# g's low half on GpSimd, Strassen's products in three pieces, and batch 0's row sums as products with ones, in a fused block-causal attention and gated feed-forward kernel

## The chip, the cores and the metric

The kernel runs on one core of a Trainium2 chip. The metric is the device time of one execution in microseconds (us); the kernel before was run three times: 994.45 us in the median, 994.39 to 995.16.

The engines are named as in the profile: PE (TensorE, matrix products; PEld its weight loads), DVE (VectorE), ACT (ScalarE), POOL (GpSimd), SP (SyncE, which only issues DMAs).

## The reference

Block-causal attention over 8 batches of 8 heads (576 tokens, head size 64, blocks of 64), then a feed-forward layer with a gate, all in float32:

```python
scores = scale * np.matmul(q, k.transpose(0, 1, 3, 2))          # q, k, v: (8, 8, 576, 64)
scores = np.where(block_i >= block_j, scores, -1000000000.0)    # blocks of 64 tokens
scores = scores - np.max(scores, axis=-1, keepdims=True)
attn = np.exp(scores)
attn = attn / (np.sum(attn, axis=-1, keepdims=True) + 1e-09)
x = np.matmul(attn, v)                                          # then heads side by side: (4608, 512)
h = x @ w_in                                                    # w_in: (512, 2048)
g = h * np.clip(h + 3.0, 0.0, 6.0) / 6.0
out = g @ w_out                                                 # w_out: (2048, 512)
```

## The kernel before, in words

**Precision.** Most products are made of three float16 products: each operand is split into a high half and a low half (the rounding rest, scaled), and high x high, high x low and low x high are summed in PSUM. Making a low half is one instruction, `scalar_tensor_tensor` (value times scale minus high half), on DVE; the high half is a scaled copy on ACT or DVE. Batch 0 runs in float32 instead, while the weights are still being loaded and split.

**Attention.** The heads go in pairs n (4 pairs a batch, 32 in all), the nine blocks of 64 queries in three groups g of three. For the pairs of batch 0, `s_pair32` and `s_soft32` make the scores (tile sf), DVE takes the row maximum (st), ACT takes the exponential (tile pf, with the row's sum as its accumulator output, `sums`), `t_block32` transposes on PE (pt, copied to pT) and `pv_group32` multiplies P^T with V (the output is also called pf). There the sums, which lie one to a partition, have to be spread along the free dimension: their reciprocals are put on a diagonal (rd, three small copies on POOL or ACT), and a product of rd with a matrix of ones in two of its quadrants (`halves`, or `cross` for the blocks whose two heads are swapped) gives pr, which is copied to rb and multiplied with pf. For the other batches `s_group` does the same with float16 halves: tiles s, p (exponentials), phl (halves of P, transposed by DMA) and pv in `pv_group`. A memset on POOL clears the half block behind p.

**Feed-forward.** The 4608 rows of x are cut into 13 pieces pc of 384 columns (pieces 0 and 3 have 192), which lie transposed in four buffers xb. For each piece and each of 16 columns f of 128 hidden units, `ffn1` makes h (24 products of 384 columns, 64 output rows each, two at a time), ACT makes r = relu(scaled h + 3), DVE r = min(r, 6) x h, ACT or DVE the high half of g, DVE its low half; `ffn2` multiplies with w_out into three tiles o, LAG = 3 columns later in the program. At the end of a piece ACT or DVE evacuates o to osb, which SP stores.

**Strassen.** In the pieces of STR = (11, 12), `h_pair` makes two columns f from seven products m of half the size instead of eight: 84 products of 192 columns in place of 48 of 384. The sums of quarters of x (`x_comb`) and of the weights (`w_comb`, once, tile ws) are made ahead; the weight sums lie in buffers that attention uses until then (`SW_TAGS`), and pieces in STR start when all attention for all of them is done (`fills`). The seven products are put together by DVE, seven instructions and one copy (hf, hu), before ACT can make r.

**The order.** The kernel does not issue its instructions as it makes them. `Recorder` records each with a due time (`key`, from tables such as AT for attention and FT for the feed-forward), what it depends on, and the engines that could do it; `schedule` then simulates five engines with estimated costs and lets each engine take, among what is ready, what is due first. `emit` issues the result (all from line 520, so the profile tells instructions apart by their tiles). Each engine then works through its own list in that order, and an instruction that waits holds up all behind it on its engine.

## Time and profile before

| what | value |
|---|---|
| median of three runs | 994.45 us |
| the profiled execution's own time | 995.16 us |
| its span, first to last instruction | 993.4 us |
| PE busy | 970.4 us, 98% |
| DVE busy | 889.6 us, 90% |
| ACT busy | 638.6 us, 64% |
| POOL busy | 67.8 us, 7% |
| read from and written to HBM | 45.09 MB, 9.44 MB |

A row that groups instructions ("lines") names the tiles as out<-in without buffer numbers, then the shapes and the count (x), then busy us and the mean ns of one, then the idle time of the engine ahead of them and what ended it. A row of the chain or of the timeline begins with start and length in us from the span's start; x24 counts instructions in the row. A row of waits names who waited for whom, then us in total, times, and the longest. Matmul ends are modelled, so a row of products may reach into the next one by some 0.2 us: where products are costed, it is from one row's start to the next row's.

### The profile page before, as it was taken

How to read it: one execution, taken by the hardware profiler on the slowest of the kernel's cores; microseconds unless marked ns; L12 is line 12 of the kernel's file. 1: busy time of each engine (PE TensorE's matmuls, PEld its weight loads, DVE VectorE, ACT ScalarE, POOL GpSimd, SP SyncE). 2: the span in 40 equal slices, each digit the busy share in tenths (PEclk: the TensorE clock that was granted, in tenths of full speed). 3: DMA queues.
4: the chain of work that ended last, by engine and by line, in shares of the span. 5: the costliest groups of instructions: out<-in, count | busy, mean ns of one | idle time of the engine just before them, and what ended most of it. 6: DMA issues, size and time to landing. Idle time of an engine off the chain costs nothing. (4 is left out here: it accounts for less than half of the span.)

```text
span 993.4 us, 31344 instructions
## 1 busy us (share of the span) xinstructions
PE 970.4 (98%) x12673; PEld 723.0 (73%) x12673; DVE 889.6 (90%) x2441; ACT 638.6 (64%) x1538; POOL 67.8 (7%) x239
## 2 busy tenths in 40 slices
PE   6899999999999999999999999999999999999998
PEld 5566667767778877777677777777667777788876
DVE  5898999999999999999999889899898889976863
ACT  4788887766757776776776665666656555354442
POOL 1132210000000000000000000000000002000000
PEclk9999999999999999999999999999999999999999
DMA  8965479899869989789998876786756551000000
GB/s 235 304 205 164 97 123 147 147 172 197 156 109 204 164 153 156 147 159 165 149 182 137 142 149 111 123 164 120 130 138 110 92 103 36 2 34 2 34 2 33
DMA packets 407041, 129.05 MB, mean 130 GB/s; under 512 B 393968, under 2 KB 396272, under 8 KB 406896
## 3 DMA queue, kind: packets, MB, share of 16 engines
q1 hardware_dynamic: 360528, 111.49, 58.9%
q10 hardware_dynamic: 46368, 15.55, 7.1%
q8 instruction: 99, 1.62, 0.7%
q14 instruction: 46, 0.38, 0.1%
HBM read 45.09 MB, written 9.44 MB: 55 GB/s over the span
## 5 line engine op out<-in xcount | busy, mean ns | idle before, releaser
L520 PE MATMUL o<-wout,g 128*64 128x512 f16 (+3 forms) x3336 | 411.1, 378 | 0.0
L520 PE MATMUL h<-x,win 128*64 128x384 f16 (+2 forms) x3952 | 361.7, 319 | 2.1 <-DVE g L520 0.9
L520 PEld LDWEIGHTS <-win 128*64 128x64 f16 (+1 forms) x4440 | 269.0, 110 | 62.7 <-issue 2.9
L520 PEld LDWEIGHTS <-g 128*64 128x64 f16 x3360 | 217.8, 110 | 106.1
L520 ACT ACTIVATE p<-s,st,esc 128x64 f32<-128x64 f32 (+1 forms) x280 | 162.8, 587 | 75.0 <-DVE st L520 62.6
L520 ACT ACTIVATE r<-h,eg,sh 128x384 f32<-128x384 f32 (+1 forms) x192 | 111.6, 599 | 51.6 <-PE h L520 47.9
L520 DVE SCALAR_TENSOR_TENSOR phl<-p,st,phl 128x128 f16<-128x128 f32 (+4 forms) x252 | 135.5, 582 | 0.1
L520 ACT ACTIVATE g<-r 128x384 f16<-128x384 f32 (+1 forms) x156 | 79.1, 507 | 69.2 <-DVE r L520 66.8
L520 DVE TENSOR_REDUCE st<-s 128x1 f32<-128x64 f32 (+1 forms) x280 | 116.9, 446 | 1.2 <-PE s L520 1.1
L520 DVE SCALAR_TENSOR_TENSOR g<-r,g 128x384 f16<-128x384 f32 (+1 forms) x192 | 102.5, 534 | 7.1 <-ACT g L520 5.6
L520 DVE SCALAR_TENSOR_TENSOR r<-r,eg,h 128x384 f32<-128x384 f32 (+1 forms) x160 | 93.9, 587 | 14.2 <-ACT r L520 13.7
L520 PE MATMUL s<-qkT 128*64 128x64 f16 (+7 forms) x1120 | 94.3, 287 | 2.5 <-DVE x L520 1.7
L520 ACT ACTIVATE phl<-p,st 128x256 f16<-128x256 f32 (+4 forms) x135 | 70.6, 557 | 26.9 <-DVE st L520 15.9
L520 PEld LDWEIGHTS <-vhl 128*64 128x64 f16 x1680 | 72.8, 110 | 13.2 <-issue 3.8
L520 PEld LDWEIGHTS <-qkT 128*64 128x64 f16 x1120 | 57.6, 110 | 26.9 <-issue 6.8
L520 PE MATMUL pv<-pT,vhl 128*64 128x192 f16 (+2 forms) x1680 | 73.2, 233 | 1.8 <-DVE x L520 0.8
L520 POOL MEMSET p<- 128x64 f32 x140 | 21.2, 152 | 593.9 <-DVE phl L520 531.0
L520 ACT ACTIVATION_READ_ACCUMULATOR p<-s,st,esc 128x1 f32 x280 | 55.5, 198 | 0.0
L520 ACT ACTIVATE r<-hf,eg,sh 128x192 f32<-128x192 f32 (+1 forms) x48 | 25.5, 591 | 43.2 <-DVE hf L520 43.2
L520 DVE TENSOR_SCALAR phl<-p,st 128x512 f16<-128x512 f32 (+4 forms) x117 | 45.2, 420 | 2.0
L520 DVE SCALAR_TENSOR_TENSOR qks<-qk,rs_q,qks 128x576 f16<-128x576 f32 x56 | 44.8, 815 | 0.0
L520 PE MATMUL m<-x,ws 128*64 128x192 f16 x768 | 35.2, 246 | 0.0
(193 smaller groups left out, 1033.0 us busy)
## 6 DMA issues: line engine op xcount, KB each, us to landing
out_dram<-osb SPq DMA_DIRECT2D x35, 256.0 KB, 2.4
qk<-in_q_dram SPq DMA_DIRECT2D x21, 288.0 KB, 3.8
rawo<-in_moe_w_out_dram SPq DMA_DIRECT2D x10, 512.0 KB, 5.6
vnat<-in_v_dram ACTq DMA_DIRECT2D x36, 128.0 KB, 4.0
qk<-in_k_dram SPq DMA_DIRECT2D x15, 288.0 KB, 4.3
qk<-in_k_dram ACTq DMA_DIRECT2D x13, 288.0 KB, 4.6
vnat<-in_v_dram SPq DMA_DIRECT2D x28, 128.0 KB, 2.9
rawi<-in_moe_w_in_dram SPq DMA_DIRECT2D x6, 512.0 KB, 5.5
```

The lines of the kernel that those rows point to most:

```text
L520: getattr(eng, method)(*args, **kw)
```

## The change

**Row sums.** `s_soft32` no longer takes the exponentials' accumulator output. In `pv_group32` the loop that makes pf runs twice: first with ones (64 columns, `full1`) as the weights into pr, then with V into pf. pr then holds the row sums at the place where pf has its rows; one instruction on DVE or ACT adds 1e-9 and copies it to rb, and DVE takes the reciprocal there (192 columns). sums, ident2, halves, cross and rd go.

**g.** r is scaled through the tables of constants, so that g's high half is a plain copy and its low half a plain difference. From piece 2 on this difference is a `tensor_tensor` on POOL.

**Strassen.** STR is (10, 11, 12). There are five buffers xb, the weight sums use other buffers, and hu uses those of phl2.

**Order.** The tables of due times have other numbers, each group of operations has a shift of its own (`SHIFT`, some 1450 numbers), and the estimated costs differ for POOL; the copies for which POOL was one of several choices now all fall to DVE and ACT.

The diff, cut to its core:

```diff
-STR = (11, 12)
-SK, SKD, XK = 19.373, 8.522, 32.06
+RDB = 3
+GLO = ("P",)
+STR = (10, 11, 12)
+SK, SKD, XK = 23.677, 8.167, 30.349
...
+SHIFT = {
+    0: 118, 2: -43, 3: -76, 4: -56, 5: 114, 6: -70, 7: 29, 8: -137, 11: -65, 12: -176, 13: -47, 14: 115,
...
+    def minus(self, out, a, b, engines):
+
+        self.add([
+            ("vector" if e == "V" else "gpsimd", "tensor_tensor", (out, a, b), dict(op=ALU.subtract))
+            for e in engines
+        ])
...
+            op.grp = self.grp + (10000 if eng == "tensor" else 20000 if ways[0][1] == "dma_start" else 0)
+            op.key += 0.1 * SHIFT.get(op.grp, 0)
...
-            port = len(wide) > 1
+            port = False
...
-            occ = 75 + (2.0 if method == "tensor_tensor" else 1.1) * n
+            occ = 80 + (1.4 if method == "tensor_scalar" else 3.2) * n
...
-    xb = [wpool.tile([P, 2, NDT, TP], F16, tag=f"x{i}", name=f"x{i}") for i in range(4)]
+    xb = [wpool.tile([P, 2, NDT, TP], F16, tag=f"x{i}", name=f"x{i}") for i in range(5)]
...
-            for i, f in enumerate((1.0, 3.0, 6.0)):
+            for i, f in enumerate((E_G, 3.0 * E_G, 6.0 * E_G)):
...
-        for ci, (c0, c1, ps) in enumerate(pss):
-            nc.scalar.activation(
-                pr[:, c0:c1], ps[:, :c1 - c0], AF.Exp, bias=st[:, 0:1], scale=1.0,
-                accum_out=st[:, 2:3] if ci else sm_,
-            )
-        if len(pss) == 2:
-            nc.vector.tensor_add(sm_, sm_, st[:, 2:3])
+        for c0, c1, ps in pss:
+            nc.scalar.activation(pr[:, c0:c1], ps[:, :c1 - c0], AF.Exp, bias=st[:, 0:1], scale=1.0)
...
-        r = sums.pop((n, g))
-        nc.vector.tensor_scalar(r, r, 1e-9, 1.0, op0=ALU.add, op1=ALU.mult)
-        nc.vector.reciprocal(r, r)
-        rd = sm.tile([P, GB, BLK], F32, tag="rd", bufs=2, name=f"rd{n}_{g}")
-        for i in range(GB):
-            nc.scaled(rd[:, i], ident2, r[:, i:i + 1], RDW)
...
-        nc.joint = "pr", n, g
-        for w, b0, b1 in sets:
-            nc.tensor.matmul(
-                pr[:, b0 * BLK:b1 * BLK], (halves, cross)[w], rd[:, b0:b1].rearrange("p i x -> p (i x)"),
-                start=True, stop=True,
-            )
...
+        for what, to in (("pr", pr), ("pf", ps)):
+            nc.joint = what, n, g
+            for w, b0, b1 in sets:
...
+                        nc.tensor.matmul(
+                            to[h * D:(h + 1) * D, i0 * BLK:b1 * BLK],
+                            vnat[n % NVB][:kp, j, h, :] if what == "pf" else full1[:kp],
+                            t[:kp, us, o:o + BLK],
...
+        nc.add([
+            ("scalar", "activation", (rb, pr, AF.Identity), dict(bias=tiny)),
+            ("vector", "tensor_scalar", (rb, pr, 1e-9, 1.0), dict(op0=ALU.add, op1=ALU.mult)),
+        ][::-1])
+        nc.vector.reciprocal(rb, rb)
...
-        nc.scaled(g[:, 0, :w], r[:, :w], E_G, "AV")
-        nc.vector.scalar_tensor_tensor(
-            g[:, 1, :w], r[:, :w], E_G, g[:, 0, :w], op0=ALU.mult, op1=ALU.subtract
-        )
+        nc.scaled(g[:, 0, :w], r[:, :w], 1.0, "AV")
+        nc.minus(g[:, 1, :w], r[:, :w], g[:, 0, :w], GLO[(pc * NFT + f) % len(GLO)] if pc > 1 else "V")
```

What this does to the engines' lists is shown at three places. First PE, at the end of pair 0's batch-0 attention, group 2 (pr0_2 and pf0_2; sf1 are the scores of pair 1, h0_4 a column of piece 0, gs1 belongs to the weights' scales). Before:

```order
L520 MATMUL pr0_2_306<-rd0_2_305,halves_95 128x128
L520 MATMUL pr0_2_306<-rd0_2_305,cross_96 128x64
L520 MATMUL h0_4_316<-x0_81,win_85 128x192 x2
L520 MATMUL sf1_3_0_296<-qkf1_123 64x256 x2
L520 MATMUL sf1_4_0_297<-qkf1_123 64x320 x2
L520 MATMUL gs1_283<-wm1_281,unit_98 64x2 x2
...
L520 MATMUL pf0_2_308<-pT0_2_275,vnat0_100 64x128 x8
L520 MATMUL pf0_2_308<-pT0_2_275,vnat0_100 64x64 x10
```

And now:

```order
L690 MATMUL pr0_2_284<-pT0_2_256,unit_96 64x128 x8
L690 MATMUL pr0_2_284<-pT0_2_256,unit_96 64x64 x10
L690 MATMUL sf1_5_0_296<-qkf1_120 64x384 x2
L690 MATMUL sf1_6_0_297<-qkf1_120 64x448 x2
L690 MATMUL gs1_261<-wm1_259,unit_96 64x2 x2
...
L690 MATMUL h0_4_290<-x0_81,win_86 128x192 x3
L690 MATMUL pf0_2_285<-pT0_2_256,vnat0_99 64x128 x8
L690 MATMUL pf0_2_285<-pT0_2_256,vnat0_99 64x64 x10
```

Two products with rd have become 18 with pT, the same 18 as those of pf, and they stand as far ahead of pf as before.

Second POOL, in the attention of pair 17 (p17 and phl17 are memsets for it, g4 the subtractions for piece 4). Before:

```order
L520 MEMSET p17_0_1346 128x64
L520 MEMSET p17_2_1348 128x64
L520 MEMSET p17_4_1369 128x64
L520 MEMSET phl17_1_1372 128x256
L520 MEMSET p17_6_1389 128x64
L520 MEMSET p17_8_1390 128x64
```

And now:

```order
L690 MEMSET p17_0_1290 128x64
L690 MEMSET p17_2_1292 128x64
L690 TENSOR_TENSOR g4_14_1264<-r4_14_1263,g4_14_1264 128x384
L690 TENSOR_TENSOR g4_13_1253<-r4_13_1252,g4_13_1253 128x384
L690 MEMSET phl17_1_1320 128x256
L690 MEMSET p17_4_1317 128x64
L690 MEMSET p17_6_1336 128x64
L690 TENSOR_TENSOR g4_15_1278<-r4_15_1277,g4_15_1278 128x384
L690 TENSOR_TENSOR g5_0_1285<-r5_0_1283,g5_0_1285 128x384
L690 MEMSET p17_8_1337 128x64
```

The subtractions stand between memsets that wait for DVE to have read the buffer's last contents. Over the whole program POOL has 176 subtractions, 160 of 384 columns and 16 of 192.

Third DVE, around column 4 of piece 5 (r5_4; st are the scores' maxima and scales, qks the halves of q and k, x the halves of x). Before:

```order
L520 SCALAR_TENSOR_TENSOR r5_4_1336<-r5_4_1336,eg8_723,h5_4_1335 128x384
L520 SCALAR_TENSOR_TENSOR x3_84<-pv16_0_1339,x3_84 128x384
L520 TENSOR_SCALAR st17_0_1344<-st17_0_1344,esc17_1296 128x3
L520 TENSOR_SCALAR pw_q18_1359<-am_q18_1361 128x2
L520 TENSOR_REDUCE st17_1_1365<-s17_1_0_0_1366 128x1
L520 SCALAR_TENSOR_TENSOR g5_4_1337<-r5_4_1336,g5_4_1337 128x384
```

And now:

```order
L690 SCALAR_TENSOR_TENSOR r5_4_1328<-r5_4_1328,eg8_688,h5_4_1327 128x384
L690 TENSOR_SCALAR qks19_1362<-qks19_1362 128x2x9x32
L690 TENSOR_SCALAR x2_83<-pv17_0_1346 128x384
L690 TENSOR_SCALAR st18_0_1351<-st18_0_1351 128x3
...
L690 SCALAR_TENSOR_TENSOR x2_83<-pv17_0_1346,x2_83 128x384
```

DVE no longer makes g's low half, and attention is one pair further on (18 and 19 in place of 17 and 18) at the same column of the feed-forward.

More of the change, by code (lines that the diff above doesn't have):

```diff
@@ L592, in pow2_scale @@
         else:
-            pw, rs = (sm.tile([P, n], F32, tag=f"{x}{n}_{nm[0]}", name=f"{x}_{nm}") for x in ("pw", "rs"))
+            pw, rs = (
+                sm.tile([P, n], F32, tag=f"{x}{n}_{nm[0]}", bufs=5 if nm[0] == "v" else 3, name=f"{x}_{nm}") for x in ("pw", "rs")
+            )
         am = sm.tile([P, n], F32, tag=f"am{n}", name=f"am_{nm}")
@@ L628 @@
     make_identity(tc.nc, ident)
-    ident2 = wpool.tile([P, BLK], F32, tag="ident2", name="ident2")
-    nc.vector.tensor_add(ident2, ident[:, :BLK], ident[:, BLK:])
-    halves = wpool.tile([P, P], F32, tag="halves", name="halves")
-    nc.gpsimd.memset(halves, 0.0)
-    for h in range(2):
-        nc.gpsimd.memset(halves[h * BLK:(h + 1) * BLK, h * BLK:(h + 1) * BLK], 1.0)
-    cross = wpool.tile([P, P], F32, tag="cross", name="cross")
-    nc.gpsimd.memset(cross, 1.0)
-    for h in range(2):
-        nc.gpsimd.memset(cross[h * BLK:(h + 1) * BLK, h * BLK:(h + 1) * BLK], 0.0)
     one = wpool.tile([P, 1], F32, tag="one", name="one")
@@ L970, in qk_prep32 @@
         nc.scaled(qT[:, c0:c1], pss[1][:, :c1 - c0], D ** -0.5, "AV")
-    sums = {}
     pf = {}
@@ L1097, in pv_group32 @@
         nj = (3 * g + 2) // 2 + 1
[L1098 to L1115 removed]
+        for what, to in (("pr", pr), ("pf", ps)):
+            nc.joint = what, n, g
+            for w, b0, b1 in sets:
+                js = [j for j in range(nj) if 2 * j - 3 * g < b1]
+                for j in js:
+                    i0 = max(b0, 2 * j - 3 * g)
+                    kp = BLK if 2 * j + 1 > 3 * g + 2 else P
+                    a = i0 * NU[g] + j
+                    us = slice(a, a + (b1 - 1 - i0) * NU[g] + 1, NU[g])
+                    for h in range(2):
+                        o = (h ^ w) * BLK
+                        nc.tensor.matmul(
+                            to[h * D:(h + 1) * D, i0 * BLK:b1 * BLK],
+                            vnat[n % NVB][:kp, j, h, :] if what == "pf" else full1[:kp],
+                            t[:kp, us, o:o + BLK],
+                            start=(j == 0),
+                            stop=(j == js[-1]),
+                        )
+            nc.joint = None
+        rb = sm.tile([P, GT], F32, tag="rb", bufs=2, name=f"rb{n}_{g}")
+        nc.add([
[3 more added lines that the diff above has]
+        nc.vector.reciprocal(rb, rb)
         if g == 0:
@@ L1256, in pv_group @@
         for pc, *_ in parts:
-            while done1 < (pc - 3) * NFT or pc == 2 and done1 < NFT or pc == 3 and done2 < NFT:
+            while (
+                done1 < (pc - 4) * NFT or pc == 2 and done1 < NFT or pc == 3 and done2 < NFT
+                or pc == 5 and done2 < 2 * NFT
+            ):
                 ffn_step(TOT)
@@ L1319, in h_plain @@
     def h_plain(pc, f):
-        x, w, fc = xb[pc % 4], width(pc), f * P % NH
+        x, w, fc = xb[pc % 5], width(pc), f * P % NH
         ps = ps_h.tile([P, TP], F32, tag="h", name=f"h{pc}_{f}")
@@ L1348, in w_comb @@
     def w_comb(c):
-        r = attp.tile([P, NDT, NH], F32, tag="qks", bufs=1, name=f"wr{c}")
-        plus(r, win[:, c, :, 0], win[:, c, :, 1])
+        rs = []
+        for i in range(2):
+            r = attp.tile([P, NDT, P], F32, tag="vhl", bufs=2, name=f"wr{c}_{i}")
+            plus(r, *(win[:, c, :, l, i * P:(i + 1) * P] for l in range(2)))
+            rs += [r[:, :2], r[:, 2:]]
+        a11, a12, a21, a22 = rs
         o = attp.tile([P, 4, 2, P], F32, tag="phl1", bufs=1, name=f"wq{c}")
-        a11, a12, a21, a22 = (r[:, 2 * j:2 * j + 2, i * P:(i + 1) * P] for i in range(2) for j in range(2))
         nc.vector.tensor_add(o[:, 0], a21, a22)
@@ L1358, in w_comb @@
         tag = SW_TAGS[c]
-        pool = {"qk": natp, "raw": ffp}.get(tag, attp)
+        pool = natp if tag == "qk" else attp
         bufs = 2 if tag in ("qk", "qkT", "pT2") else 1
@@ L1732 @@
                 left[pc] += 1
-    for _, _, f, a, key in sorted(ev, key=lambda e: e[:2]):
-        nc.key, nc.cls = key, "w" if f in (load_next, maxes, splits) else "a"
+    for _, no, f, a, key in sorted(ev, key=lambda e: e[:2]):
+        nc.key, nc.cls, nc.grp = key, "w" if f in (load_next, maxes, splits) else "a", no
         f(*a)
```

106 lines of the change are left out of this document (43 added, 63 removed), and 153 rows, old and new, of the table SHIFT.

## The prediction

> **What bounds the kernel now.** I read the busy time of each engine by stretch first, then PE's waits, then the chain that ended last. The columns are start and end of a stretch, its length, then PE, PEld, DVE, ACT and POOL in busy us with the number of instructions, the granted clock (1.00 throughout), the DMA share and GB/s:
>
> ```profile
> 0.00:50.00 50.00, 37.42 (x452) 27.93 (x454) 37.05 (x108) 28.89 (x91) 8.92 (x36) 1.00 0.91 270
> 50.00:250.00 200.00, 196.03 (x2218) 133.12 (x2216) 192.42 (x557) 155.11 (x378) 27.55 (x67) 1.00 0.78 157
> 250.00:850.00 600.00, 597.40 (x7873) 450.49 (x7871) 560.71 (x1548) 396.41 (x956) 31.38 (x137) 1.00 0.76 136
> 950.00:993.40 43.40, 39.59 (x582) 30.38 (x577) 21.68 (x51) 15.00 (x27) 0.00 (x0) 1.00 0.06 20
> ```
>
> PE is idle for 12.6 us of the first 50, for 4.0 us of the next 200, for 2.6 us of the 600 after that, and for 3.8 us at the end, where the last result is evacuated and stored. So PE's own work sets the time, and an edit counts by what it adds to or takes from PE, and by what it does to some 19 us of waits. DVE has little room: 93% busy from 250 to 850 us. PE's longest waits:
>
> ```profile
> PE qt L520 <- DMA qf<-in_q_dram: 4.9, 2, 4.4
> PE sf L520 <- ACT pf L520: 3.7, 3, 1.5
> PE s L520 <- DVE x L520: 1.7, 2, 1.4
> PE pt L520 <- ACT pT L520: 1.4, 1, 1.4
> PE pt L520 <- ACT pf L520: 1.3, 2, 1.1
> ```
>
> The first is the load of q, which the change cannot shorten. The others of batch 0 end with ACT's exponentials (pf) or copies (pT); the one on x ends with DVE, later in the run.
>
> **Strassen for piece 10.** The chain of waits is, in its second half, PE alone, and so shows what a block of products costs:
>
> ```profile
> 858.35 1.95 PE h L520 x24
> 866.13 3.47 PE m L520 x84
> 869.60 3.88 PE o L520 x36
> ```
>
> Two columns f of h cost 2 x 1.95 = 3.90 us as 48 products, and 3.47 us as the 84 half-width products of Strassen's scheme. Piece 10 has eight such pairs: PE loses 8 x 0.43 = 3.4 us, all on the path.
>
> **Row sums of batch 0 on PE.** The new sums are the products of pf once more, with ones in place of V, so their cost is that of pf (the times are from a row's start to the next block's start); the old broadcast pr goes:
>
> ```profile
> 27.75 0.81 PE L520 MATMUL pf<-pT,vnat 128*64 128x128 f32 x12
> 28.50 0.28 PE L520 MATMUL mb_v<-dg_v,one 1*64 1x1 f32 x4
> 28.70 0.49 PE L520 MATMUL pr<-rd,halves 128*128 128x128 f32 x2
> ...
> 29.29 0.58 PE L520 MATMUL sf<-qkf,qkf 64*64 64x128 f32 x8
> ```
> ```profile
> 46.39 1.11 PE L520 MATMUL pf<-pT,vnat 128*64 128x64 f32 x20
> 47.33 0.60 PE L520 MATMUL o<-wout,g 128*64 128x256 f32 x4
> ```
> ```profile
> 54.75 0.39 PE L520 MATMUL pr<-rd,halves 128*128 128x128 f32 x2
> ...
> 55.14 0.87 PE L520 MATMUL h<-x,win 128*128 128x192 f32 x4
> ...
> 57.70 1.82 PE L520 MATMUL pf<-pT,vnat 128*64 128x128 f32 x36
> 59.45 0.33 PE L520 MATMUL pt<-ident,pf 128*128 128x128 f32 x1
> ```
>
> A group of g=0 costs 0.75 us, of g=1 0.94, of g=2 1.75; the old pr costs 0.39 to 0.59 us, 0.49 in the middle. The four pairs' g=0 groups add 4 x (0.75 - 0.49) = 1.0 us, but lie in the first 40 us, where PE idles 12.6 us anyway: I count them at nothing, and 1.0 us if that idle time goes. The other eight groups add 4 x (0.94 + 1.75 - 2 x 0.49) = 6.8 us between 45 and 135 us, where PE has almost no idle time: all of it counts.
>
> What goes with the old sums is on the other engines:
>
> ```profile
> L520 ACT ACTIVATION_READ_ACCUMULATOR pf<-sf,st 128x1 f32 x40 | 8.0, 199 | 0.0
> L520 ACT ACTIVATE rd<-ident,sums 128x64 f32<-128x64 f32 x14 | 4.2, 338 | 0.8 <-DVE sums L520 0.5 <-ACT rb L520 0.3
> ```
>
> ACT loses 40 reads of its accumulator, 8.0 us, and 14 of the diagonal copies rd, 4.2 us; POOL loses the other 22. Such a read stands between each exponential and the transposition that PE waits for. In the first 50 us 12.6 - 4.9 = 7.7 us of PE's idle time are not the first load. The five ended by pf become shorter by at least a read, 5 x 0.2 = 1.0 us; in the other direction all 7.7 us could go. What comes next there is DMA (0.91 busy), so not all of it. I take 5.0 us, most of the 3.7 + 1.3 + 1.4 = 6.4 us that end with ACT, since the groups also lose ACT's and POOL's steps ahead of pr; this is the least certain term. New on DVE are 12 reciprocals of 192 columns. No row shows one over three columns; bounded by the 0.35 us of another 192-column instruction (hf, below) and eight times that, they are 4 to 34 us of DVE, behind a product that nobody on PE waits for soon. I take the lower end.
>
> **g's low half on GpSimd.** The chain of a g, and what four GpSimd subtractions' nearest kin (xr, an addition of the same size) took:
>
> ```profile
> L520 DVE SCALAR_TENSOR_TENSOR g<-r,g 128x384 f16<-128x384 f32 x176 | 96.8, 551 | 6.6 <-ACT g L520 5.1
> L520 DVE SCALAR_TENSOR_TENSOR r<-r,eg,h 128x384 f32<-128x384 f32 x144 | 87.3, 607 | 13.2 <-ACT r L520 12.8
> L520 ACT ACTIVATE r<-h,eg,sh 128x384 f32<-128x384 f32 x112 | 74.4, 666 | 39.2 <-PE h L520 37.5 <-DMA out_dram<-osb 1.3
> L520 ACT ACTIVATE g<-r 128x384 f16<-128x384 f32 x142 | 74.0, 521 | 65.4 <-DVE r L520 63.1
> L520 DVE SCALAR_TENSOR_TENSOR hf<-m,hu 128x192 f32<-128x192 f32 x48 | 15.5, 354 | 3.8 <-PE m L520 0.8
> L520 DVE SCALAR_TENSOR_TENSOR x<-xt,x 128x384 f16<-128x384 f32 x8 | 5.1, 638 | 0.0
> L520 POOL TENSOR_TENSOR xr<-x x4: 1022/1622/3038, 795.8 to 838.4; 128x384 f32<-128x384 f16 x4
> ```
>
> 160 of the 176 wide subtractions leave DVE: 160 x 0.551 = 88 us (16 narrow ones too). Piece 10's assembly brings 7 x 8 x 0.354 = 20 us back. DVE is not the bound, so this saves nothing by itself. It pays for something else: Strassen's weight sums lie in buffers of the attention, so attention must now be done before three Strassen pieces rather than two. One such piece is 8 x (3.47 + 3.88) = 59 us, so DVE has 541 us in place of 600 for what it does from 250 to 850 us. That work is 560.7 us less 120 subtractions (7.5 pieces), 66 us, less piece 10's own r, 16 x 0.607 = 10 us: 485 us, 90% of 541.
>
> Sharing has a price, seen at two of the four additions:
>
> ```profile
> 835.41 4.02 POOL L520 TENSOR_TENSOR xr<-x 128x384 f32<-128x384 f16 x2 [5.12 <-DVE x L520]
> ...
> 838.12 0.54 DVE L520 TENSOR_TENSOR xt<-xt,xr 128x192 f32<-128x192 f32 x1
> 838.59 1.26 DVE L520 SCALAR_TENSOR_TENSOR x<-xt,x 128x384 f16<-128x384 f32 x1
> ```
>
> ```profile
> 827.64 0.75 DVE L520 SCALAR_TENSOR_TENSOR phl<-p,st,phl 128x512 f16<-128x512 f32 x1
> ```
> ```profile
> 829.96 0.89 DVE L520 SCALAR_TENSOR_TENSOR phl<-p,st,phl 128x512 f16<-128x512 f32 x1
> ```
>
> While POOL adds, DVE's x takes 1.26 us, where its mean is 0.64, and its xt 0.54 where 192 columns cost 0.35. The phl that starts inside another addition takes 0.89 us, the one before it 0.75. That is 0.95 us over the four additions, 0.24 us each; and POOL itself needs 1.0 to 3.0 us. With 0.24 us more for each of 120, 29 us, DVE is at 514 us of 541, 95%, little more than now. So the 6.6 us of PE's idle time between 50 and 850 us stay about as they are; I take 2.8 us off, since the waits on DVE's x and g sit in front of the relief, with 0 and 6.6 as ends.
>
> The Trainium skill ("GPSIMD Engine Reference", When to use GPSIMD) speaks against the move: two-input elementwise work belongs on VectorE, GpSimd being about half as fast. The rows agree (1.0 to 3.0 us against 0.55); by itself that rule costs PE nothing, as long as g is early enough.
>
> **The sum.** -3.4 + 6.8 - 5.0 - 2.8 = -4.4 us. The profiled execution took 995.16 us for its span of 993.4, so 990.8; the median of the runs lies 0.7 us lower, so **990.0 us**. With the first two terms fixed and the others uncertain by half their size, this case's own range is 986 to 992.5. About 0.2%, 2 us, is what a measurement of this kernel can tell from no change.
>
> **Rivals.** (1) Slower: g comes late. The chain is 0.67 + 0.61 + 0.52 = 1.80 us up to the high half, then 0.55 us now, up to 3.04 on POOL, where it also queues behind memsets that wait for DVE's phl. In PE's order, priced at the rates above, every g of pieces 2 to 12 now has at least 5.7 us of other products between its h and its first use; after the change 14 of 176 have under 5.5, the least 4.3. With three hand-overs of some 0.3 us (half an instruction in front), the chain is 1.8 + 0.9 + POOL's time: it decides from 2.3 us of POOL on, and at 3.04 makes PE wait 0.7 us in each of 14 places, +10 us: 1000. Against it: the middle xr is 1.6 us, and 110 of the 176 uses are over 10 us away. Chance 0.16. (2) No change: the start is set by its loads, and none of the 5.0 us comes: 995. For it speaks the DMA share of 0.91 there. Chance 0.17. (3) More gain: all 7.7 and 6.6 us of idle time go: 983. Chance 0.11. (4) DVE is held by POOL: at the longest hold seen, 1.26 - 0.64 = 0.62 us for each of 120, DVE needs 485 + 74 = 559 us of 541, and is the bound by 18 us: 1008; it decides from 0.47 us on. Against it: the four held DVE for 0.24 us in the mean. Chance 0.10. The Trainium skill ("SBUF — State Buffer", Who interferes with whom) has this as a rule: a VectorE instruction with two SBUF inputs and a GpSimd instruction that reads SBUF exclude each other, for whole instructions, whoever starts first. By it, the case comes out whenever DVE's next instruction of that kind arrives early in a subtraction.
>
> **How the numbers follow.** The forecast has 0.46. Faster: 0.46 + 0.11 = 0.57; same, rival 2: 0.17; slower: 0.16 + 0.10 = 0.26. The range 982 to 1001 takes in the forecast, rival 2 and the times worked out for 1 and 3, and leaves out 4 and the outer edges of 1 and 3, some 0.2 in all.
>
> **What would show it.** Right: PE does 24 x 84 products m; PE busy in the first 50 us rises above 40; pr costs as much as pf; POOL's g under 2.3 us in the mean and no line of PE waiting for POOL; DVE 90 to 95% busy until attention ends, some 60 us further from the end than now. Wrong: PE waits named on POOL's g (rival 1), DVE at 99% with long phl and x instructions (4), or a first 50 us as idle as before (2).

## The result: slower by 38 us

The changed kernel takes 1032.57 us in the median of four runs (1028.92 to 1038.04), the kernel before 994.42: a ratio of 1.0389, 95% interval 1.0363 to 1.0416. The forecast was 990 us, its range ended at 1001.

The profiled execution took 1030.56 us, its span 1028.8. The busy time by stretch, with the columns as in the prediction (the last stretch now ends at 1028.8):

```profile
0.00:50.00 50.00, 38.98 (x414) 28.04 (x414) 34.62 (x86) 22.23 (x57) 2.07 (x18) 0.86 0.82 240
50.00:250.00 200.00, 192.21 (x2261) 133.75 (x2259) 188.85 (x527) 148.60 (x337) 9.81 (x40) 1.00 0.74 148
250.00:850.00 600.00, 583.58 (x7771) 427.15 (x7768) 560.56 (x1481) 395.20 (x969) 147.29 (x263) 1.00 0.82 140
950.00:1028.80 78.80, 74.93 (x1144) 58.74 (x1138) 39.51 (x102) 29.69 (x55) 18.64 (x20) 1.00 0.06 22
```

PE's idle time from 50 to 850 us has grown from 6.6 to 24.2 us (7.8 + 16.4), and besides the clock is down to 0.86 in the first 50 us. Over the whole span the engines were busy for:

```profile
PE 988.4 (96%) x13185; PEld 727.9 (71%) x13185; DVE 885.4 (86%) x2351; ACT 635.3 (62%) x1495; POOL 203.6 (20%) x366
```

So of the 35.4 us by which the span grew, 17.4 are idle time of PE (40.4 us, 23.0 before), and 18.0 are busy time (988.4 us, 970.4 before). Idle time alone shows half of the loss. No single wait explains it. PE's longest waits now:

```profile
PE s L690 <- ACT p L690: 6.4, 8, 3.1
PE sf L690 <- ACT qkf L690: 4.5, 2, 3.8
PE qt L690 <- DMA qf<-in_q_dram: 3.3, 1, 3.3
PE h L690 <- DVE r L690: 2.7, 4, 1.5
PE pv L690 <- ACT p L690: 2.2, 3, 1.2
```

There are many small ones on attention's chain (s, p, x), and none of PE for POOL's g (PE's weight loads waited for it once, for 0.4 us). Now the groups that the prediction spoke of. PE's row sums, before and after:

```profile
L520 PE MATMUL pr<-rd,halves 128*128 128x128 f32 (+1 forms) x24 | 5.0, 291 | 0.0
L520 PE MATMUL pr<-rd,cross 128*128 128x64 f32 (+1 forms) x24 | 4.4, 266 | 0.0
```
```profile
L690 PE MATMUL pr<-pT,unit 128*64 128x128 f32 (+2 forms) x272 | 16.0, 263 | 0.0
```

DVE's low half of P, before and after, with the new reciprocals, and POOL's subtraction:

```profile
L520 DVE SCALAR_TENSOR_TENSOR phl<-p,st,phl 128x128 f16<-128x128 f32 (+4 forms) x252 | 135.5, 582 | 0.1
```
```profile
L690 DVE SCALAR_TENSOR_TENSOR phl<-p,st,phl 128x256 f16<-128x256 f32 (+4 forms) x252 | 146.3, 622 | 2.0 <-ACT phl L690 1.7
L690 DVE RECIPROCAL rb<-rb 128x192 f32<-128x192 f32 x12 | 16.2, 1348 | 1.9 <-ACT rb L690 1.9
```
```profile
L690 POOL TENSOR_TENSOR g<-r,g 128x384 f16<-128x384 f32 (+1 forms) x176 | 173.1, 989 | 427.1 <-ACT g L690 309.6 <-DVE g L690 55.2 <-DVE pw_q L690 12.7
```

phl has grown from 582 to 622 ns. A reciprocal of 192 columns takes 1.35 us. POOL's subtraction takes 0.99 us in the mean, far below the 2.3 us from which rival 1 decides.

Where does a longer phl come from? From POOL: here is one subtraction, and the phl that VectorE began while it ran (start and length in us):

```profile
255.37 1.36 POOL L690 TENSOR_TENSOR g<-r,g 128x384 f16<-128x384 f32 x1 [5.29 <-DVE phl L690]
```
```profile
255.88 1.40 DVE L690 SCALAR_TENSOR_TENSOR phl<-p,st,phl 128x512 f16<-128x512 f32 x1
```

POOL ends at 256.73, and phl 0.55 us later. The one of the same size that the prediction shows by itself took 0.75 us, this one 1.40: it stood for most of the time for which POOL still ran.

**Theories.** A: the 38 us come through VectorE, which POOL's subtractions hold and which has the reciprocals besides, in stretches where it has no room; PE pays in many small waits. B (rival): the new order itself is at fault, packed so that usual chains come late. C (my prediction's): the reciprocals cost nothing. D: the clock at the start is a part. The expectations split some of these (A1, A2, A', D') and add E, transfers that come late. All results, each against the kernel before on the same chip:

| kernel | what it is | us, median (lowest to highest) | ratio, 95% interval |
|---|---|---|---|
| constant_for_difference | changed, POOL writes zeros | 1010.85 (1009.57 to 1012.62) | 1.0165 (1.0146 to 1.0185) |
| eight_columns | changed, POOL subtracts 8 columns | 1012.96 (1012.10 to 1013.18) | 1.0176 (1.0153 to 1.0199) |
| one_input | changed, POOL scales r | 1017.66 (1014.45 to 1021.46) | 1.0236 (1.0191 to 1.0280) |
| low_half_on_dve | changed, low half on VectorE | 1017.62 (1015.61 to 1019.56) | 1.0226 (1.0202 to 1.0249) |
| before_gpsimd | before, with the subtraction on POOL | 998.38 (996.63 to 999.34) | 1.0038 (1.0024 to 1.0052) |
| copy_for_reciprocal | changed, no reciprocals | 1022.23 (1020.62 to 1026.11) | 1.0284 (1.0256 to 1.0312) |
| no_row_sums | and few products for row sums | 1020.35 (1019.62 to 1022.74) | 1.0257 (1.0234 to 1.0281) |
| before_row_sums | before, with the new row sums | 1026.04 (1023.34 to 1029.65) | 1.0321 (1.0294 to 1.0348) |
| before_row_sums_const | and no reciprocals | 1021.87 (1019.97 to 1025.53) | 1.0281 (1.0258 to 1.0303) |
| all_three | changed: zeros, no reciprocals, few products | 1006.10 (1002.16 to 1009.16) | 1.0108 (1.0072 to 1.0143) |
| dve_no_row_sums | the same with the low half on VectorE | 1010.17 (1007.93 to 1010.39) | 1.0154 (1.0138 to 1.0170) |
| all_three_no_stores | all_three, 33 stores left out | 996.59 (991.28 to 999.78) | 1.0014 (0.9994 to 1.0034) |
| all_three_filled | all_three, early transpositions twice | 998.63 (998.09 to 999.76) | 1.0046 (1.0029 to 1.0063) |
| start_filled | changed, 11 idle products at the start | 1029.79 (1025.92 to 1031.57) | 1.0349 (1.0321 to 1.0378) |
| after_filled | changed, early transpositions twice | 1028.80 (1027.27 to 1032.23) | 1.0356 (1.0332 to 1.0380) |
| dve_filled | low_half_on_dve, the same | 1013.82 (1013.41 to 1014.54) | 1.0200 (1.0185 to 1.0215) |
| no_shift | changed, SHIFT empty | 1062.25 (1057.03 to 1065.58) | 1.0678 (1.0642 to 1.0714) |

### The profile page after: what moved, and what is told of

It is laid out like the page before. It is cut to its first block, busy times and chain, and to the rows that moved or that the text cites. A ratio compares the mean times of both kernels' runs of the same rounds, so it can differ in the third digit from the quotient of the medians.

```text
span 1028.8 us, 32511 instructions
## 1 busy us (share of the span) xinstructions
PE 988.4 (96%) x13185; PEld 727.9 (71%) x13185; DVE 885.4 (86%) x2351; ACT 635.3 (62%) x1495; POOL 203.6 (20%) x366
## 5 line engine op out<-in xcount | busy, mean ns | idle before, releaser
L690 PE MATMUL h<-x,win 128*64 128x384 f16 (+2 forms) x3568 | 328.2, 318 | 3.8 <-DVE r L690 2.7
L690 POOL TENSOR_TENSOR g<-r,g 128x384 f16<-128x384 f32 (+1 forms) x176 | 173.1, 989 | 427.1 <-ACT g L690 309.6
L690 ACT ACTIVATE p<-s,st,esc 128x64 f32<-128x64 f32 (+3 forms) x280 | 163.1, 587 | 53.4 <-DVE st L690 41.4
L690 DVE SCALAR_TENSOR_TENSOR phl<-p,st,phl 128x256 f16<-128x256 f32 (+4 forms) x252 | 146.3, 622 | 2.0 <-ACT phl L690 1.7
L690 DVE TENSOR_REDUCE st<-s 128x1 f32<-128x64 f32 (+3 forms) x280 | 118.0, 444 | 4.6 <-PE s L690 4.4
L690 PE MATMUL s<-qkT 128*64 128x512 f16 (+7 forms) x1120 | 99.1, 288 | 9.7 <-ACT p L690 6.4
L690 ACT ACTIVATE phl<-p,st 128x128 f16<-128x128 f32 (+4 forms) x144 | 76.2, 566 | 39.9 <-DVE st L690 19.5
L690 ACT ACTIVATE r<-hf,eg,sh 128x384 f32<-128x384 f32 (+1 forms) x64 | 36.0, 618 | 63.3 <-DVE hf L690 61.9
L690 PE MATMUL m<-x,ws 128*64 128x192 f16 x1152 | 56.4, 246 | 1.5 <-DVE hu L690 0.8
L690 PEld LDWEIGHTS <-ws 128*64 128x64 f16 x1152 | 50.8, 110 | 5.1 <-issue 1.4
```

The costliest lines, as they stand in the source:

```text
L690: getattr(eng, method)(*args, **kw)
```

## Experiments on GpSimd's subtraction

Most edits stand in `emit`, behind the making of the order, so that every instruction keeps its place.

**constant_for_difference.**

```diff
             for method, args, kw in o.ways[o.eng][0]:
+                if o.eng == "gpsimd" and method == "tensor_tensor":
+                    method, args, kw = "memset", (args[0], 0.0), {}
                 getattr(eng, method)(*args, **kw)
```

> The changed kernel with every instruction in its place, but GpSimd writes zeros where it subtracted, so g's low half is left out of the result; GpSimd no longer reads SBUF there and no longer waits for g's high half. Theory A (VectorE is held by the subtractions: its instructions grew by 34 us in all, 28 of them from attention's phl, st, x, qks and the like, in a stretch where it is 97 to 99% busy): most of that growth goes, phl back from 622 to about 582 ns, and 12 to 20 us of the 38 with it, 1012 to 1020 us. Theory B (the new order packs TensorE's list so tightly that ScalarE's and VectorE's usual chains come late, whoever shares SBUF): 1029 to 1036 us, as the changed kernel's 1032.6.

1010.9 us: 21.7 us less, as A said and B did not. phl is back where it was before:

```profile
L692 DVE SCALAR_TENSOR_TENSOR phl<-p,st,phl 128x256 f16<-128x256 f32 (+4 forms) x252 | 135.8, 582 | 3.3 <-ACT phl L692 2.9
```

VectorE's busy time, with the same 2351 instructions, is 844.6 us instead of 885.4: the holds were 40.8 us, 0.23 us for each of 176 subtractions.

```profile
PE 980.7 (97%) x13185; PEld 729.2 (72%) x13185; DVE 844.6 (84%) x2351; ACT 633.7 (63%) x1495; POOL 99.5 (10%) x366
```

PE's busy time falls by 7.7 us too, with the same 13185 products. A product's row is longer than PE's pace (a row of h is 326 ns long, but 24 of them take 1.95 us, 81 ns each), so a shorter wait between two products leaves no idle time. That the 7.7 us are such waits is inferred.

**eight_columns.**

```diff
+                if o.eng == "gpsimd" and method == "tensor_tensor":
+                    eng.tensor_tensor(*(a[:, :8] for a in args), **kw)
+                    method, args, kw = "memset", (args[0][:, 8:], 0.0), {}
```

> The changed kernel with every instruction in its place, but GpSimd's subtraction is cut to 8 of its 384 (or 192) columns, and a memset writes zeros to the others, so most of g's low half is left out. GpSimd still waits for g's high half, as it did, and TensorE still waits for GpSimd; only the time in which GpSimd reads SBUF goes. Theory A (the hold, as long as GpSimd's instruction reads): as with the constant, 1008 to 1014 us, with phl at 585 to 595 ns. Rival (what the constant took away was the wait of TensorE for a low half that came late): near the changed kernel, 1028 to 1036 us.

1013.0 us. POOL waits for g's high half as in the changed kernel and PE for POOL, and still 19.6 us are gone: it is the hold, not a late low half. Nor is it the clock: that was 0.989 to 0.995 in these runs, 0.991 in the mean as in the changed kernel's (0.984 to 0.995). phl is short here too:

```profile
L693 DVE SCALAR_TENSOR_TENSOR phl<-p,st,phl 128x256 f16<-128x256 f32 (+4 forms) x252 | 135.9, 582 | 3.2 <-ACT phl L693 3.0
```

**one_input.**

```diff
+                if o.eng == "gpsimd" and method == "tensor_tensor":
+                    method, args, kw = "tensor_scalar", (args[0], args[1], 2.0 ** -12, 1.0), dict(op0=ALU.mult, op1=ALU.mult)
```

> The changed kernel with every instruction in its place, but GpSimd scales r (one input of 384 columns from SBUF) where it subtracted g's high half from r (two inputs), so the low half is another number. If an instruction of GpSimd that reads SBUF at all holds VectorE, the holds per instruction stay in proportion to its length, phl stays over 600 ns, and the time lies between 1015 and 1036 us by how long GpSimd's instruction is; if only two inputs hold it, phl comes to 582 to 590 ns and the time to 1008 to 1014 us.

1017.7 us, between the two: POOL's instruction took 0.63 us instead of 0.99, phl 590 ns, VectorE was busy for 856.9 us. One input holds too, but by 12.3 us in all (856.9 - 844.6) against 40.8, less than in proportion to POOL's time. Neither expectation was quite right.

**low_half_on_dve.** One edit, `GLO = ("V",)`, and the order worked out anew.

> The changed kernel with g's low half back on VectorE for all pieces, the order worked out anew with the same tables; row sums and three pieces of Strassen's products stay. VectorE gets 160 x 0.55 = 88 us and loses the holds, 28 to 34 us. Theory A1 (the holds and their scatter are what hurts, since they come when VectorE can't catch up): as fast or faster, 1005 to 1028 us. Theory A2 (VectorE's sum of work before attention's end is what sets the time): some 54 us more work in a stretch with no room, slower than the changed kernel, 1050 us or more. Theory B (the order): nothing can be said within 20 us, since the order is another.

1017.6 us: 15 us faster than with GpSimd, though VectorE's busy time rises from 885.4 to 912.7 us. The order is another one, so that the 15 us by themselves prove little, as B has it; but A2's 1050 us and more can be left aside. From 250 to 600 us VectorE is denser than in the kernel before and in the changed one, busy for 345 of 350 us, and PE waits only 3.4 us:

```profile
250.00:600.00 350.00, 346.63 (x4740) 261.36 (x4738) 345.05 (x1005) 235.87 (x594) 15.52 (x90) 1.00 0.97 161
```

So it is not the sum of VectorE's work that hurts. This fits A1, scattered holds in an order that hadn't counted on them: here the order was made with the subtractions on VectorE.

**before_gpsimd.** In the kernel before, POOL subtracts for pieces 2 to 12, at the time at which VectorE did.

```diff
+                if method == "scalar_tensor_tensor" and (self.low & {id(args[0])}):
+                    eng, method, args, kw = self.nc.gpsimd, "tensor_tensor", (args[0], args[1], args[3]), dict(op=ALU.subtract)
...
-            for i, f in enumerate((1.0, 3.0, 6.0)):
+            for i, f in enumerate((E_G, 3.0 * E_G, 6.0 * E_G)):
```

> The kernel before, every instruction in its place, with one part of the change: from piece 2 on GpSimd subtracts for g's low half, at the time at which VectorE did. VectorE loses 88 us and gains holds of 0.22 us for each of 176, 38 us, so it has 50 us less to do, and attention isn't drawn together. Theory A (the holds hurt because the change spent VectorE's room on an attention that ends earlier, and left none where they fall): with the room kept, no loss, 990 to 997 us. Theory A' (a hold costs TensorE wherever it falls, since it lengthens the chains that TensorE waits for): slower by 5 to 20 us, 1000 to 1014. My prediction's rival 1 (g late): the same 1000 to 1014, but with waits of TensorE on GpSimd's g.

998.4 us, 3.6 us more than before, a little above A's range and below A'. The holds are as large as in the changed kernel:

```profile
L523 DVE SCALAR_TENSOR_TENSOR phl<-p,st,phl 128x128 f16<-128x128 f32 (+4 forms) x252 | 144.7, 622 | 1.1 <-ACT phl L523 0.4
```

And yet the move as a whole costs 3.6 us, where in the changed kernel the holds alone cost 21.7, and the move, by low_half_on_dve, 15. The stretch from 250 to 600 us shows the difference; before, before with POOL, changed, and changed with zeros (columns as above):

```profile
250.00:600.00 350.00, 349.19 (x4742) 262.52 (x4740) 334.36 (x958) 244.31 (x598) 15.26 (x86) 1.00 0.87 155
```
```profile
250.00:600.00 350.00, 348.33 (x4726) 262.03 (x4724) 323.16 (x874) 244.05 (x597) 86.95 (x165) 1.00 0.86 154
```
```profile
250.00:600.00 350.00, 337.76 (x4626) 245.62 (x4624) 338.13 (x924) 240.27 (x604) 84.19 (x167) 1.00 0.98 162
```
```profile
250.00:600.00 350.00, 344.79 (x4750) 249.85 (x4747) 325.66 (x951) 246.63 (x624) 42.87 (x170) 1.00 0.99 167
```

Before, VectorE was busy for 334 of 350 us (96%), and PE waited 0.8 us. With POOL, VectorE drops to 323 us (92%), and PE waits 1.7. In the changed kernel attention is drawn together, VectorE is at 338 (97%), and PE waits 12.2 us; without the holds, at 326 (93%), 5.2. VectorE's share alone doesn't decide: it was 96% before and 99% in low_half_on_dve, with 0.8 and 3.4 us of waits. Neither do holds that the order hadn't counted, which cost little here. The 12.2 us stand where both come together.

## Experiments on the row sums

**copy_for_reciprocal.**

```diff
+                if method == "reciprocal" and self.count(args[0]) == 192:
+                    method, args, kw = "tensor_scalar", (args[0], args[1], 0.0, 0.01), dict(op0=ALU.mult, op1=ALU.add)
```

> The changed kernel with every instruction in its place, but the 12 reciprocals of 192 columns (1.35 us each) become a multiplication and an addition of the same size that writes a constant, so batch 0's rows are not divided by their sums. Theory A (what VectorE has too much of in batch 0's stretch is paid by TensorE): VectorE loses 12 x 1.0 us or more, and the time falls by 6 to 10 us, to 1023 to 1027. Theory C (my prediction's: the reciprocals stand behind products that nobody on TensorE waits for soon): no more than 2 us, 1030 to 1033. Theory B says the same as C.

1022.2 us: without the twelve reciprocals it is 10.3 us less. The clock was a little higher as well, 0.994 in the mean of the runs for 0.991, some 3 us of 1030 if it counts in full (an estimate), so that some 7 us are the reciprocals' own. C falls. They take 16.2 us of VectorE in the stretch in which batch 0's attention is worked off; its phl instructions up to 250 us (busy time, then their number) before the change, in the changed kernel, and here:

```profile
0.00:250.00 250.00, 32.36 (x69) 1.00 0.81 179
```
```profile
0.00:250.00 250.00, 26.86 (x56) 0.97 0.76 167
```
```profile
0.00:250.00 250.00, 31.89 (x65) 0.99 0.78 174
```

Of the 13 phl of 69 by which attention is behind by then, 9 are back without the reciprocals; a part of that can be the clock's, which is 0.99 in this stretch for 0.97 (the third number from the end).

**no_row_sums.** Besides that, of each group's products pr only those with `start` are issued.

```diff
+            if o.eng == "tensor" and calls[0][0] == "matmul" and str(calls[0][1][0].tensor.name).split("/")[-1][:2] == "pr":
+                calls = [(m, a, dict(k, stop=True)) for m, a, k in calls if k["start"]]
```

> The changed kernel with every instruction in its place, but of each group's products for the row sums only those that open a region are left (4 of 6 to 18, about what the old broadcast cost), and the 12 reciprocals are replaced by a constant, so batch 0 isn't divided by its sums. What it saves beyond the 10.3 us of the reciprocals alone is the price of the new products on TensorE. My prediction's term was 6.8 us there (7.8 with the first groups): 1014 to 1016 us by it. If the waits on VectorE hide the products: 1019 to 1023 us.

1020.4 us, 1.9 less than without reciprocals alone; the intervals overlap. So the price of the products in this order isn't told from nothing. It speaks against the 6.8 us of the prediction; that the products fill waits which PE has anyway is inferred.

**before_row_sums.** The kernel before with `s_soft32` and `pv_group32` of the changed one; the order is worked out anew with the old tables.

> The kernel before with one part of the change: batch 0's row sums as products with ones, with the 12 reciprocals of 192 columns. The order is worked out anew with the old tables. My prediction's terms for this part, +6.8 on TensorE and -5.0 at the start: 996 us. By the runs so far (10.3 us for the reciprocals, 2 to 7 for the products, nothing won at the start): 1006 to 1012 us.

1026.0 us, 31 more than before, far above every expectation.

**before_row_sums_const.** That kernel with the edit of copy_for_reciprocal.

> The kernel before with the row sums as products with ones alone (1026.0 us), every instruction in its place, with a constant for the 12 reciprocals. If the reciprocals cost in this order what they cost in the changed one: 1014 to 1018 us. What remains above the kernel before is then the products (6.8 us by their sum) and an order with old tables, 17 us longer by the scheduler's estimate. If the reciprocals cost here nothing, as in my prediction: 1024 to 1028 us.

1021.9 us: 4.2 less in the medians, but the intervals of the ratios overlap, so that the price of the reciprocals in the old order stays open. The other 27 us are not taken apart: the products' 6.8, tables that were made for another program, and the clock are in them. The clock alone, 0.59 for 25 us in the profile of this kernel, is 10 us by estimate:

```profile
25.00:50.00 25.00, 19.02 (x144) 12.00 (x141) 14.77 (x46) 10.47 (x24) 2.16 (x4) 0.59 0.77 249
```

## Experiments on what is left

**all_three.** The edits of constant_for_difference, copy_for_reciprocal and no_row_sums at once.

> The changed kernel with every instruction in its place, with three things taken out at once: GpSimd writes zeros in place of the subtraction, a constant stands for the reciprocals, and of the row sums' products only those that open a region are left. If holds, reciprocals and products are the whole of the loss and add up: 1032.6 - 21.7 - 10.3 - 7 = 993 to 995 us, a little above what the third piece of Strassen's products would leave of the kernel before (991). If they overlap, since one wait hides another: 997 to 1006. If the order costs something by itself: over 1000.

1006.1 us. Singly the three saved 33.9 us, together 26.5: they overlap, and some 12 us remain above the kernel before. In its trace ACT stands for a store whose buffer it needs (first row), and PE with it (second):

```profile
322.97 0.51 ACT L697 ACTIVATE r<-h,eg,sh 128x192 f32<-128x192 f32 x1 [3.94 <-DMA out_dram<-osb]
```
```profile
324.74 0.58 PE L697 MATMUL s<-qkT 128*64 128x448 f16 x2 [4.27 <-ACT p L697]
```

r and osb share the buffers `stage`. The scores behind r wait in ACT's queue, and PE waits for them. At the end of this stop the granted clock falls for a while (the eighth column):

```profile
320.00:325.00 5.00, 0.73 (x10) 0.48 (x8) 1.24 (x4) 1.88 (x6) 0.26 (x1) 0.89 1.21 297
325.00:330.00 5.00, 5.00 (x66) 4.15 (x64) 3.56 (x12) 3.20 (x9) 0.15 (x1) 0.76 0.83 150
```

So the two may not be separate costs: a late transfer leaves PE idle, and the clock fell behind that. The changed kernel has the same stop, though its clock stayed at 1.00 there:

```profile
335.51 1.05 ACT L690 ACTIVATE r<-h,eg,sh 128x192 f32<-128x192 f32 x2 [2.70 <-DMA out_dram<-osb]
```

**dve_no_row_sums.** low_half_on_dve without reciprocals and with few products.

> The kernel with the low half on VectorE (1017.6 us), every instruction in its place, with a constant for the reciprocals and only the products for the row sums that open a region. What is left of the change is the third piece of Strassen's products and the order that goes with it. If the parts add up: 1017.6 - 12.2 = 1005 us, which is some 15 us more than the 991 that the third piece alone should give, and as much is then left in the order; if VectorE's extra 50 us of work count where the reciprocals were: 1008 to 1013; if nothing but holds and row sums was wrong: 990 to 996.

1010.2 us, 7.4 less than low_half_on_dve: most of the 12.2 us that the same two edits took from the changed kernel shows here too.

**all_three_no_stores.**

```diff
+            if calls[0][0] == "dma_start" and not self.on_chip(calls[0][1][0]):
+                self.stores = getattr(self, "stores", 0) + 1
+                if self.stores <= 33:
+                    continue
```

> As all three taken out at once (1006.1 us), and besides the first 33 of the 51 stores of the output are left out, so that about the first nine pieces are never written; the rest is in its place. In the run with all three out, ScalarE stood for 3.9 us behind a store of the output whose buffer it needed, and for 5 us behind maxima that waited for a load of k, and TensorE with it for 4.4 and 3.7 us; the DMA engines were busy for 1.0 of the stretch from 250 to 400 us. Theory E (what is left over is the packed order's short lead on transfers): the first of these stops goes, the second becomes shorter: 998 to 1002 us. Rival (what is left over is the slower clock at the start and many small waits): 1004 to 1008 us.

996.6 us, 9.5 less. No wait for a store is left, and that of the maxima for k is shorter; in all_three and here:

```profile
DVE qkmx L697 <- DMA qk<-in_k_dram: 3.8, 1, 3.8
```
```profile
DVE qkmx L701 <- DMA qk<-in_k_dram: 2.5, 1, 2.5
```

Transfers that come late in the packed order are a part of the rest (E). The clock was higher here as well, 0.995 to 1.000 for 0.991 to 0.997. At equal clocks the gain is smaller: at 0.995 999.3 and 999.8 us here and 1005.4 there, at 0.997 999.0 and 1002.2, so 3 to 6 us.

**all_three_filled.**

```diff
                 getattr(eng, method)(*args, **kw)
+                if method == "transpose" and o.start < 45e3:
+                    for _ in range(1):
+                        eng.transpose(*args, **kw)
```

> As all three taken out at once (1006.1 us), and besides each of batch 0's transpositions on TensorE in the first 45 us is done twice (some 25 more products of 0.2 us, 5 us of TensorE's 12 idle us there); the rest is in its place. Theory D' (the clock falls where TensorE does little over some 10 us; the runs at a clock of 0.991 to 0.995 would lose up to 5 us to it): clock 0.998 to 1.00, 1001 to 1005 us. Rival (the clock's falls don't hang on that, or the time lost lies in stretches that wait anyway): clock as before, 1006 to 1011 us, later by what the extra products delay.

998.6 us, 7.5 less, with *more* work for PE. The clock of its runs was 0.996 to 0.998; all_three's was 0.991 to 0.997. That is the way that D' has it, and further than its 1001 to 1005 us. The clock can be half of it, by estimate: 0.004 more in the mean of the runs is 4 us of 1000. Something else moved too: ACT's longest wait for a store was 2.9 us for 3.9 in all_three. The two aren't told apart. In the changed kernel the clock falls to a half from 25 to 40 us:

```profile
20.00:25.00 5.00, 3.79 (x63) 2.84 (x65) 4.55 (x11) 4.38 (x13) 0.00 (x0) 1.00 0.99 276
25.00:30.00 5.00, 5.00 (x49) 3.55 (x45) 4.23 (x10) 1.68 (x6) 0.15 (x1) 0.53 1.06 374
30.00:35.00 5.00, 5.00 (x45) 3.31 (x44) 3.91 (x11) 2.93 (x7) 0.00 (x0) 0.50 0.98 281
35.00:40.00 5.00, 4.01 (x16) 1.72 (x16) 3.82 (x9) 2.90 (x10) 0.51 (x2) 0.61 0.63 194
```

**start_filled.** 3 transpositions of the identity ahead of the first load's arrival and 8 ahead of the first scores, into the tiles that are written next.

> The changed kernel with 11 more products of no use on TensorE in its idle time at the start: 3 ahead of the first load's arrival and 8 between the first transpositions and the first scores, where it waited 3.8 us; the rest is in its place. In the changed kernel the granted clock was 0.5 to 0.6 from 25 to 40 us, and 0.984 to 0.995 in the mean of its four runs, 1.00 before the change. Theory D (the clock falls because TensorE did too little in the first 25 us): clock 1.00, the time falls by 5 to 9 us to about 1024 to 1027, and the four runs, which lay 9 us apart, come within 2 us. Rival (the fall comes from something later, or is chance): clock as before, 0.98 to 1.00, 1029 to 1038 us.

1029.8 us with clocks of 0.991 to 1.000: D as I put it then, too little work for PE at the start, isn't shown by products that fill the first 10 us. The one run at 1.000 was the fastest, 1025.9.

**after_filled.** The changed kernel with the edit of all_three_filled, nothing left out.

> The changed kernel itself, nothing left out, with each of batch 0's transpositions on TensorE in the first 45 us done twice, the rest in its place. With holds, reciprocals and products out, the same edit raised the clock from 0.991-0.997 to 0.996-0.998 and took 7.5 us off. If that is a part of the changed kernel's loss too: clock 0.996 or more, 1024 to 1028 us, and runs within 3 us of each other. If holds and reciprocals hide it: 1030 to 1036 us.

1028.8 us, clock 0.993 to 0.998. That is 3.8 us less in the medians, but the intervals of the ratios overlap: not shown.

**dve_filled.** low_half_on_dve with that edit.

> The same edit to the kernel with the low half on VectorE (1017.6 us at a clock of 0.989 to 0.997), nothing left out. This is the best version of the change that these runs point to. If the two gains add up: 1009 to 1013 us, still 15 us or more above the kernel before; if VectorE's waits hide the clock: 1015 to 1019.

1013.8 us at 0.998 to 1.000, the best version of the change that leaves nothing out, and still 20 us slower than before. No run points to a version that beats both.

**no_shift.** `SHIFT = {}`.

> The changed kernel with all of the 1450 shifts of the order's due times at zero, and nothing else changed. The scheduler's own estimate for its order grows with that by 17 us. If the chip follows the estimate: 1049 us. If what the shifts won is eaten by what the estimate leaves out (holds, reciprocals), so that the packed order and the loose one lose the same time to VectorE: 1028 to 1040 us. If the shifts themselves do the harm (theory B): below 1028.

1062.3 us. B in its plain form falls: the shifts save 30 us. What the order gets wrong is what it was made for. Its estimate for VectorE (`68 + 1.042 * n`) gives a reciprocal of 192 columns 268 ns, where the row has 1348; and `port = False` counts no hold of a two-input instruction by GpSimd.

## Why the prediction was wrong, point by point

**What bounds the kernel.** PE's own work; that stayed so, but its busy time rose by 18.0 us, where I had counted 6.8 - 3.4 = 3.4. The products themselves are as counted: those for row sums are 16.0 us busy, where the two groups of the old pr had 5.0 + 4.4: 6.6 us more, near the 6.8 that I had. The slow clock adds some 7 us (0.14 x 50, an estimate). The 7.8 us that are left (18.0, plus Strassen's 3.4, less 6.6 and 7.0) are about the 7.7 that go with zeros from POOL: by the same inference as there, small waits that don't show as idle time.

**g's low half: the step that failed most.** Its numbers came out, in part by luck. The hold was put at 0.24 us, from four additions of 1.8 us in the mean, and is 0.23 for subtractions of 0.99. VectorE's load was put at 514 of 541 us; from 250 us to the end of attention's phl it is 513.65 of 551, with more of attention left at 250 us than I had assumed:

```profile
250.00:801.00 551.00, 537.40 (x7188) 393.59 (x7186) 513.65 (x1398) 377.21 (x937) 131.59 (x250) 1.00 0.89 152
```

The step from there failed: "95%, little more than now. So the 6.6 us of PE's idle time between 50 and 850 us stay about as they are". The mean share didn't tell what PE waits: the holds fell on an order that hadn't counted them and had little room (97% from 250 to 600 us). Idle time didn't fall by 2.8 us, it rose by 17.6, and eight_columns and constant_for_difference show that 19.6 to 21.7 us of time hang on the holds. Rival 4 had the mechanism, but a wrong point from which it decides: 0.47 us each, where the sum of the work passes the stretch. It decided at 0.23, without VectorE being full. The Trainium skill ("SBUF — State Buffer", Who interferes with whom), which stood beside that rival, was the better guide: the pair of rows at 255 us agrees with its rule.

**The reciprocals.** I bounded them by 4 to 34 us, took the lower end and had nobody wait. They took 16.2 us of VectorE, and the kernel is 10.3 us faster without them, some 7 by themselves. The failed step is "behind a product that nobody on PE waits for soon": each stands in VectorE's queue, and behind it other work of attention for which PE does wait.

**Row sums on PE, +6.8.** Right as work. As price it was too high here by the medians, 1.9 us, which the runs can't tell from nothing.

**The start, -5.0.** Nothing of it came as time. PE is busy for 38.98 us of the first 50, under the 40 that I had named: its idle time fell by 1.6 us, and the slower clock takes some 7. The reads of the accumulator are gone, and most of PE's waits on pf with them (3.7 + 1.3 us before, 0.7 + 1.0 now, in the rows of sf and pt), but a new one on qkf stands in their place:

```profile
L690 PE MATMUL pt<-ident,pf 128*128 128x128 f32 (+1 forms) x100 | 21.1, 313 | 2.8 <-ACT pf L690 1.0 <-DVE rb L690 0.6 <-ACT rb L690 0.6
L690 PE MATMUL sf<-qkf 64*64 64x64 f32 (+7 forms) x120 | 16.6, 505 | 6.2 <-ACT qkf L690 4.5 <-DVE dg_v L690 1.0 <-ACT pf L690 0.7
```

Rival 2 had that much right.

**Strassen, -3.4.** Not measured by itself. A block of 84 products m takes 3.47 us in the changed kernel's chain, as before. In the changed kernel piece 10 begins where VectorE has 46.90 of 49 us, and PE waits 2.8 of them:

```profile
801.00:850.00 49.00, 46.18 (x589) 33.56 (x585) 46.90 (x84) 17.99 (x32) 15.70 (x13) 1.00 0.04 9
```

**Rival 1** (g late) was wrong: no product of PE waits for POOL's g, and eight_columns, which keeps that wait, gives back 19.6 us.

**What I had not seen at all.** The transfers and the clock. With the three other costs taken out, leaving out stores was worth 9.5 us (3 to 6 at equal clocks), and the doubled transpositions 7.5, of which the clock can explain about half. They weren't taken out together, and the one can bring the other; how much of each is in the changed kernel's 38 us stays open, as does what makes the clock fall at the start.

## What to carry to other kernels

An engine's busy share alone doesn't say what another waits for it. VectorE at 99% of a stretch cost PE 3.4 us where the order knew the work; at 92%, with holds that the order didn't know, 1.7; at 97% with such holds 12.2. So ask of a change that lengthens instructions both whether there is room and whether the order counts them: moving the subtraction cost 3.6 us in the one kernel and some 15 in the other. Price a new instruction by its own kind before placing it "off the path", since whatever is queued behind it on its engine waits with it, and somebody waits for that. And an order that was fitted to estimated costs has to be fitted to measured ones when a change brings costs that the estimate doesn't know.

## What the runs showed of the hardware

Held by POOL's subtractions were instructions of VectorE with two inputs from SBUF, and scaled copies within SBUF (the first two rows); not held were those with one of two inputs in PSUM (the third, h) and the reciprocal. In the changed kernel and with zeros from POOL:

```profile
L690 DVE TENSOR_SCALAR phl<-p,st 128x512 f16<-128x512 f32 x31 | 17.1, 562 | 0.7 <-issue 0.5
L690 DVE TENSOR_TENSOR st<-st 128x1 f32<-128x1 f32 x60 | 13.2, 220 | 5.5 <-ACT p L690 5.1
L690 DVE SCALAR_TENSOR_TENSOR r<-r,eg,h 128x384 f32<-128x384 f32 x128 | 77.3, 605 | 6.8 <-ACT r L690 6.1 <-issue 0.2
L690 DVE RECIPROCAL st<-st 128x3 f32<-128x3 f32 x84 | 14.1, 167 | 0.4
L690 DVE TENSOR_SCALAR g<-r 128x384 f16<-128x384 f32 x34 | 11.9, 351 | 0.5 <-PE o L690 0.2
```
```profile
L692 DVE TENSOR_SCALAR phl<-p,st 128x512 f16<-128x512 f32 x31 | 14.8, 487 | 0.7 <-issue 0.5
L692 DVE TENSOR_TENSOR st<-st 128x1 f32<-128x1 f32 x60 | 9.2, 153 | 5.7 <-ACT p L692 5.4
L692 DVE SCALAR_TENSOR_TENSOR r<-r,eg,h 128x384 f32<-128x384 f32 x128 | 77.6, 608 | 14.4 <-ACT r L692 13.9
L692 DVE RECIPROCAL st<-st 128x3 f32<-128x3 f32 x84 | 14.2, 170 | 0.4
L692 DVE TENSOR_SCALAR g<-r 128x384 f16<-128x384 f32 x34 | 13.6, 401 | 1.7 <-PE o L692 0.6 <-PE mb_q L692 0.5
```

A GpSimd instruction that only writes (the memset) did not hold those with two inputs: phl is at 582 ns with zeros as before the change. This is as the Trainium skill ("SBUF — State Buffer", Who interferes with whom) states it. But memsets did lengthen VectorE's own scaled copies of g (the last row), 401 ns with zeros for 351: there POOL no longer waits for the copy and runs beside it.

A reciprocal of 192 columns takes 1.35 us where one of three takes 0.17: 6 ns a column.

The granted clock can fall on a single core. In the kernel before, and in before_gpsimd, it was 0.998 to 1.000 in every run; in the kernels with the new row sums 0.978 to 1.000, in the profiled executions by falls to a half, most of them in the first 100 us. The Trainium skill ("TensorE: Matmul & The Clock Gate", What's actually happening) ties the half clock to an idle window of some 3.4 us. The fall of all_three behind PE's gap of 4.27 us agrees; but in the changed kernel the longest gap of PE in the 5 us ahead of the fall at 25 us was 1.0 us:

```profile
24.48 0.33 PE L690 MATMUL sf<-qkf 64*64 64x64 f32 x4 [1.00 <-DVE dg_v L690]
```

Among the ten runs of all_three_no_stores the one at 1.000 took 991.3 us, those at 0.998 took 992.3 to 995.8, and those at 0.995 to 0.997 took 997.4 to 999.8.
